# Three moves in the order of VectorE's work: a held bank, a later copy, a longer hand-over

## The chip, the cores and the metric

The kernel runs on one core of a Trainium2 chip. The metric is the time on the device in microseconds (us), the median of several runs. TensorE (PE) multiplies matrices into PSUM banks; VectorE (DVE) and ScalarE (ACT) empty those banks; GpSimd (POOL) works between tiles in SBUF; SyncE (SP) issues the transfers. Each engine works through its own list of instructions in the order in which the program wrote it.

## The reference

Two branches share one input `x` of 2048 rows by 512 columns and are mixed by a gate per row:

```
g = sigmoid((x * gate_w).sum(-1))                     # one number a row
a = attention: 32 heads of width 16, one shared k and v;
    softmax(q k^T / 4) v over all 2048 rows, times wo
b = (silu(x @ w_gate) * (x @ w_up)) @ w_down          # inner width 1792
out = g * a + (1 - g) * b
```

All arrays are 32-bit floats. The 32 heads each need a 2048 x 2048 table of scores and its exponentials; that is the larger part of the work. The feed-forward branch `b` and the queries of the heads are the other part.

## The kernel before, in words

A first stage transposes `x`, splits numbers into a high and a low part (products are made of three terms to keep precision), and makes keys, values and the first queries. A last stage multiplies the attention by `wo`. Between them, from 48.1 to 1289.0 us of the span by its first and last score, lies the attention with the main loop, and the change touches only what is ordered there.

**Blocks.** The main loop first makes 16 short rounds, then one block of another form, and then blocks k = 9 to 127 (line 773). Each unit u is one head and 128 rows of keys. A block makes eight score tiles (two for each of four units, of a later part of the order) and then mixes four units (`mix`, line 665: the exponentials times the values, summed for a head in one bank, `po`). Four blocks make a head, so blocks with k = 0 mod 4 begin one. The order of a block is written out in `STEPS` (line 54): `SSFFFFSFFSFFSFFFSFFFSFFS`. An S makes a score tile, an F feeds one step of other work to TensorE. Steps are counted from 0 here, so the scores 1 to 8 are steps 0, 1, 6, 9, 12, 16, 20, 23, and the sixteen feeds stand between.

**Scores.** A score (line 646) is a pair of matmuls (line 653) on two halves of TensorE's rows into one of two `pss` buffers of two banks each. So a score needs the buffer of the score two before it. `KINDS` (line 55) says how a buffer is emptied: for A, ScalarE takes the exponential of both banks; for H, VectorE copies the second bank out (line 657), ScalarE takes the exponential of the first bank, and later that of the copy. Scores 1, 2, 3, 5 and 6 of a block are H.

**Feeds.** The other work is a list of jobs: query projections, gate and up projections of the feed-forward branch (12 matmuls of 128 rows each), and down projections (15, or 12 in the last group of a chunk). A job fills one of three `pf` banks. `Halves` (line 371) splits each matmul in two of 64 rows, a low and a high half, and runs the low half of one job beside the high half of an earlier one in the same feed (line 175). It keeps a clock: one for each feed, one for each score, 16 for a block's mix. A job's high half may begin `LAG` = 6 clocks after its low half ended; a small VectorE memset of `sign` (line 396) stands between them. When its high half has ended, the bank counts as free `SLACK` = 6 clocks later (line 404), and only then may a new job's low half start on it. No clock of the planner is a time: it only sets the order.

**The end of a job.** With a job's last matmul its `end` is called (line 181), which writes VectorE's operation on the bank: line 260 copies a gate projection out; line 287 multiplies an up projection with the gate's activation (preceded by line 277, if that is not done yet; line 289 where the activation isn't there yet); lines 322 and 324 add a down projection up; lines 208 to 232 are for queries. The functions in `after` then load the next weights. What can wait is put off to the end of the block: the activation on ScalarE (lines 269, 273), and a list `DEFER` of VectorE work with a cost for each (line 277 or 291: 0.7; the cast of the result in two parts, lines 106 and 107: 1.2). A block spends at most `BUDGET` = 3.2 of such cost, and first up to two entries of `LATER`.

**A head's sums.** When a head's last unit is mixed, its bank `po` must be copied out before the next head's first mix, four steps of mixing and eight scores later. That copy (line 690) waits in the list `COPY`, and is written in the next block as soon as two scores are made (line 724), so at step 1, behind score 2. Reciprocals and products (lines 682 to 691) follow through `LATER`.

Of the kernel before, what the change touches and what calls it, by code (L numbers as in the profile page):

```python
# [19 lines left out]
S = 2048  # L20
D = 512
H = 32
# [13 lines left out]
LIMIT = 40.0  # L36
ORDER = (0, 1, 2, 3)
GROUPS = ((0, 1, 2, 3, 4), (5, 6, 7, 8, 9), (10, 11, 12, 13))
SLACK = 6
LAG = 6  # L40
LONG = 8
GAP = 36
# [20 lines left out]
def tile_gated_mix(ctx, tc, x, wq, wk, wv, wo, w_gate, w_up, w_down, gate_w, out):  # L63
# [55 lines left out]
    wg_v = w_gate.rearrange("(k p) f -> p k f", p=P)  # L119
    wu_v = w_up.rearrange("(k p) f -> p k f", p=P)  # L120
    W, HT = {}, {}
    ACTS, DEFER, LOADS = [], [], []

    def run(queue, n):
        for _ in range(min(n, len(queue))):
            queue.pop(0)()
# [30 lines left out]
    def follow(ins, other):  # L157
        tc.add_manual_dep(getattr(ins, "ins", ins), getattr(other, "ins", other).name,
                          mybir.DependencyInfo(mybir.DependencyClass.Sync, mybir.DependencyReason.DATA), reason="rows")

    class Job:
# [4 lines left out]
        def step(self, i, half=None):  # L166
            if i == 0 and not half:
                self.ps = ps_f.tile([P, CH], F32, name="pf")
                self.terms = self.terms()
            a, b = self.terms[i]  # L170
            last = i == self.size - 1
            if half is not None:
                rows = slice(half * RT, (half + 1) * RT)
                a, b = a[rows], b[rows]
            ins = nc.tensor.matmul(self.ps, a, b, start=(i == 0 and not half), stop=(last and half != 0))  # L175
            if half == 0:
                self.lows = ins
            elif half and i == 0:
                follow(ins, self.lows)
            if last and half != 0:  # L180
                self.end(self.ps)
                for f in self.after:
                    f()
                run(LOADS, 2)


    WQ, QS, STORES = {}, {}, []

# [182 lines left out]
    class Halves:  # L371
# [6 lines left out]
        def step(self, more):  # L378
# [20 lines left out]
            if self.high:  # L399
# [3 lines left out]
                if not self.high:  # L403
                    self.free.append(self.clock + SLACK)

# [224 lines left out]
    with tc.tile_pool(name="bpool", bufs=2) as bp:  # L630
# [15 lines left out]
        def score(u, j, half=False):  # L646
            h, kt = divmod(u, NT)
            if j == 0:
                new_pt(u)
            ps = ps_s.tile([P, 2 * CH], F32, name="pss")  # L650
            for b in range(2):
                rows = slice(b * RT, (b + 1) * RT)
                nc.tensor.matmul(ps[:, b * CH:(b + 1) * CH], ks[rows, kt * P:(kt + 1) * P], QS[h][rows, j, :],  # L653
                                 start=True, stop=True)
            halves.clock += 1
            pt = PT[u][:, j * 2 * CH:(j + 1) * 2 * CH]
            other = nc.vector.tensor_copy(pt[:, CH:], ps[:, CH:]) if half else None  # L657
            return pt, ps, other

        def exps(pt, ps, other=None, w=slice(None)):  # L660
            ins = nc.scalar.activation(pt[:, w], ps[:, w], AF.Exp, scale=SCALE)  # L661
            if other is not None:
                tc.declare_no_dep(getattr(ins, "ins", ins), getattr(other, "ins", other), reason="another bank")

        def mix(u):
            h, kt = divmod(u, NT)
            pt = PT.pop(u)
            if kt == 0:
                run(COPY, 1)
                PO[:] = [ps_o.tile([P, CH], F32, name="po")]  # L670
            po = PO[0]
            for c in range(NCH):
                nc.tensor.matmul(po[c * 2 * DH:(c + 1) * 2 * DH, :], vaug[:, kt, :], pt[:, c * CH:(c + 1) * CH],  # L673
                                 start=(kt == 0), stop=(kt == NT - 1))
            if kt == NT - 1:

                osb = hp.tile([P, CH], F32, name="osb")
                rsb = hp.tile([P, CH], F32, name="rsb", bufs=1)

                def invert(i):  # L680
                    w = slice(i * P, (i + 1) * P)
                    nc.vector.reciprocal(rsb[:, w], rsb[:, w])  # L682

                def store():
                    nc.vector.tensor_tensor(osb, osb, rsb, ALU.mult)
                    for c in range(NCH):
                        nc.sync.dma_start(o_d[h * DH:(h + 1) * DH, c * CH:(c + 1) * CH],
                                          osb[c * 2 * DH:c * 2 * DH + DH, :])

                COPY.append(lambda: nc.vector.tensor_copy(osb, po))  # L690
                LATER.extend([(0.8, lambda: nc.vector.stream_shuffle(rsb, osb, [DH] * 2 * DH))] +
                             [(1.0, lambda i=i: invert(i)) for i in range(TC)] + [(0.8, store)])
# [5 lines left out]
        def feed(k, more=True):  # L698
            for _ in range(k):
                if JOBS and more or halves.busy():  # L700
                    halves.step(more)

        def block(k, first, last, steps, kinds, order):
            more = k < NB - STOP
            tiles = [(u, j) for u in range(first, last) for j in range(2)]
            order = list(order)
            made = []

            def emit():
                while order and order[0] != "|" and int(order[0][0]) < len(made):  # L710
                    i, how = int(order[0][0]), order.pop(0)[1]
                    pt, ps, other = made[i]
                    if how == "s":
                        exps(pt, pt, w=slice(CH, None))
                    else:
                        exps(pt, ps, other, slice(0, CH) if kinds[i] == "H" else slice(None))

            for i, what in enumerate(steps):
                if what == "F":
                    feed(1, more)  # L720
                elif len(made) < len(tiles):
                    made.append(score(*tiles[len(made)], kinds[len(made)] == "H"))
                    emit()
                if len(made) > 1:
                    run(COPY, 1)
            if order:
                order.pop(0)
            run(ACTS, len(ACTS))
            emit()
            assert not order and len(made) == len(tiles)  # L730
            left = BUDGET
            for queue, n in ((LATER, 2), (DEFER, len(DEFER))):
                while n and queue and queue[0][0] <= left:
                    cost, f = queue.pop(0)
                    left, n = left - cost, n - 1
                    f()
            for u in range(BLOCK * k, BLOCK * (k + 1)):
                mix(u)
            halves.clock += 2 * LONG
# [7 lines left out]
        with tc.manual_schedule():  # L747
# [25 lines left out]
            for k in range(2 * BEGIN // BLOCK, NB):  # L773
                u = BLOCK * k
                if k == 2 * BEGIN // BLOCK:
                    n = u + 6 - (u + 1)
                    block(k, u + 1, u + 6, TURN, "A" * 2 * n, [f"{i}d" for i in range(2 * n)])
                elif k == NB - 1:
                    block(k, u + 2, u + 4, STEPS, "AAAA", ("0d", "1d", "2d", "3d", "|"))
                else:  # L780
                    block(k, u + 2, u + 6, STEPS, KINDS, EXPS)
                h = u // NT
                if k % (NT // BLOCK) == 0 and 0 < h < H - 1:
                    load_head(h + 1)
                if k == NB - EARLY:
                    load_o(OUTS[0], range(KD - 1))
# [119 lines left out]
```

## Time and profile before

| | us |
|---|---|
| median of three runs | 1374.05 |
| lowest and highest run | 1371.92, 1374.65 |
| the profiled execution | 1375.02 |
| its span, first to last instruction | 1373.3 |
| TensorE busy in the span | 1342.4 (98%) |
| ScalarE busy | 1084.7 (79%) |
| VectorE busy | 867.8 (63%) |
| GpSimd busy | 388.9 (28%) |

The granted clock of TensorE is 0.996 of full speed over the span. Rows of the profile give a line of the kernel, an engine, an operation and its tiles as out<-in. A list in order of time begins each row with start and length in us, counted from the span's start; neighbouring instructions of the same kind are merged into one row with their number behind an x, and in brackets stands the idle time before the row and what ended it. A row of waits reads: who waited <- for whom, us in total, how often, the longest. The table by stretches gives, for each stretch, its length and then the busy time and number of TensorE's matmuls and weight loads. The ends of matmuls are modelled and overlap, so that a busy TensorE may still be waiting.

### The profile page before, as it was taken

Reading aid. Unit: us, or ns where it says so; the run is one execution under the profiler, and the core shown is the slowest. Engines: PE = TensorE matmul, PEld = TensorE weight load, DVE = VectorE, ACT = ScalarE, POOL = GpSimd, SP = SyncE. Lnnn points to the kernel's source line nnn. Section 1 sums busy time; section 2 is a strip of 40 time slices with the busy share of each in tenths; the row PEclk is TensorE's granted clock in tenths of the full one; section 3 lists DMA queues with packets and bytes.
Section 4 is the critical chain, followed back from the end, with each engine's and each line's share of the span. In section 5 each row is a group of like instructions: output and inputs, shape, how many; then the busy total and the mean of one; then the engine's idle time right before and its main releaser. Section 6 shows DMA issues by size and latency. Waiting matters only on the chain. (4 is left out here: it accounts for less than half of the span.)

```text
span 1373.3 us, 27568 instructions
## 1 busy us (share of the span) xinstructions
PE 1342.4 (98%) x10755; PEld 811.2 (59%) x10755; DVE 867.8 (63%) x1458; ACT 1084.7 (79%) x1699; POOL 388.9 (28%) x408
## 2 busy tenths in 40 slices
PE   9999999999999999999999999999999999999998
PEld 7655565565556555656555555655565656565576
DVE  5564677567566667577566676577566666576532
ACT  4578888888888888888888888888888888888500
POOL 6140321142131242142131241241131331332344
PEclk9999999999999999999999999999999999999999
DMA  7456211131141231121141230121221221221154
GB/s 272 144 173 195 79 35 36 41 88 43 51 135 36 66 84 41 47 74 52 51 120 43 71 85 25 58 81 36 59 66 36 81 65 33 74 72 45 44 164 140
DMA packets 101495, 107.84 MB, mean 79 GB/s; under 512 B 9968, under 2 KB 69616, under 8 KB 99696
## 3 DMA queue, kind: packets, MB, share of 16 engines
q1 hardware_dynamic: 99632, 105.81, 26.7%
q8 instruction: 89, 1.46, 0.5%
q10 hardware_dynamic: 1728, 0.20, 0.1%
q14 instruction: 46, 0.38, 0.1%
HBM read 76.09 MB, written 29.36 MB: 77 GB/s over the span
## 5 line engine op out<-in xcount | busy, mean ns | idle before, releaser
L661 ACT ACTIVATE pt<-pss 128x512 f32<-128x512 f32 (+1 forms) x1024 | 757.1, 778 | 183.5 <-PE pss L653 163.9
L657 DVE COPY pt<-pss 128x512 f32<-128x512 f32 x590 | 394.0, 688 | 299.1 <-PE pss L653 293.1
L673 PE MATMUL po<-pt,vaug 128*32 128x512 f32 x4096 | 467.6, 596 | 0.0
L653 PE MATMUL pss<-qs,ks 64*128 64x512 f32 x2048 | 437.6, 421 | 18.1 <-DVE sign L396 5.3
L661 ACT ACTIVATE pt<-pt 128x512 f32<-128x512 f32 x590 | 351.5, 630 | 1.2 <-DVE pt L657 1.2
L653 PEld LDWEIGHTS pss<-qs,ks 64*128 64x128 f32 x2048 | 206.4, 184 | 213.9 <-issue 102.1
L673 PEld LDWEIGHTS po<-pt,vaug 128*32 128x32 f32 x4096 | 119.5, 109 | 272.0 <-issue 271.7
L106 POOL CAST wgh<-wraw 128x512 fp32r<-128x512 f32 x56 | 34.7, 620 | 457.0 <-PE pf L175 368.8
L175 PE MATMUL pf<-xh,wgh 64*128 64x512 f32 (+1 forms) x444 | 164.0, 391 | 0.0
L175 PE MATMUL pf<-xh,wgl 64*128 64x512 f32 (+1 forms) x444 | 162.6, 390 | 0.0
L175 PE MATMUL pf<-xh,wuh 64*128 64x512 f32 (+1 forms) x440 | 162.1, 391 | 0.0
L175 PE MATMUL pf<-xl,wgh 64*128 64x512 f32 (+1 forms) x444 | 161.9, 391 | 0.0
L175 PE MATMUL pf<-xh,wul 64*128 64x512 f32 (+1 forms) x440 | 158.7, 390 | 0.0
L175 PE MATMUL pf<-xl,wuh 64*128 64x512 f32 (+1 forms) x440 | 156.8, 391 | 0.0
L175 PE MATMUL pf<-wdh,hh 64*128 64x512 f32 (+1 forms) x427 | 154.2, 393 | 2.3 <-DVE hh L106 2.0
L175 PE MATMUL pf<-wdl,hh 64*128 64x512 f32 (+1 forms) x427 | 155.2, 393 | 1.0 <-POOL wdl L107 1.0
L175 PE MATMUL pf<-wdh,hl 64*128 64x512 f32 (+1 forms) x427 | 154.0, 392 | 0.0
L682 DVE RECIPROCAL rsb<-rsb 128x128 f32<-128x128 f32 x128 | 116.9, 935 | 3.1 <-issue 0.8
L106 POOL CAST wuh<-wraw 128x512 fp32r<-128x512 f32 x56 | 35.9, 641 | 284.1 <-PE pf L175 248.1
L175 PEld LDWEIGHTS pf<-xh,wgh 64*128 64x128 f32 (+1 forms) x444 | 82.0, 185 | 4.8
L175 PEld LDWEIGHTS pf<-xh,wgl 64*128 64x128 f32 (+1 forms) x444 | 81.6, 185 | 4.3
L175 PEld LDWEIGHTS pf<-xh,wuh 64*128 64x128 f32 (+1 forms) x440 | 81.3, 185 | 4.5
(157 smaller groups left out, 1583.1 us busy)
## 6 DMA issues: line engine op xcount, KB each, us to landing
wraw<-in_B_w_gate_dram SPq DMA_DIRECT2D x56, 256.0 KB
wraw<-in_B_w_up_dram SPq DMA_DIRECT2D x56, 256.0 KB
wraw<-in_B_w_down_dram SPq DMA_DIRECT2D x56, 256.0 KB
qs<-q_d SPq DMA_DIRECT2D x62, 192.0 KB
q_d<-hl SPq DMA_DIRECT2D x18, 256.0 KB
q_d<-hh SPq DMA_DIRECT2D x18, 256.0 KB
o_d<-osb SPq DMA_DIRECT2D x128, 32.0 KB
a_d<-acc SPq DMA_DIRECT2D x4, 1024.0 KB
```

The source lines that it names most:

```text
L106: eng_hi.tensor_copy(hi, src)
L175: ins = nc.tensor.matmul(self.ps, a, b, start=(i == 0 and not half), stop=(last and half != 0))
L653: nc.tensor.matmul(ps[:, b * CH:(b + 1) * CH], ks[rows, kt * P:(kt + 1) * P], QS[h][rows, j, :], start=True, stop=True)
L657: other = nc.vector.tensor_copy(pt[:, CH:], ps[:, CH:]) if half else None
L661: ins = nc.scalar.activation(pt[:, w], ps[:, w], AF.Exp, scale=SCALE)
L673: nc.tensor.matmul(po[c * 2 * DH:(c + 1) * 2 * DH, :], vaug[:, kt, :], pt[:, c * CH:(c + 1) * CH], start=(kt == 0), stop=(kt == NT - 1))
L682: nc.vector.reciprocal(rsb[:, w], rsb[:, w])
```

## The change

`SLACK` goes from 6 to 7. The operation that empties a job's bank, and the functions behind it, move into a new method `leave`, which is put on a list `EVAC`. The list is run at once, except while `HOLD` is set; then it is run behind the next score, its copy included. `HOLD` is set for a feed when one of the next two steps is a score and that score is of kind H. With `STEPS` as it is, these are the feeds at steps 4, 5 (ahead of score 3), 10, 11 (ahead of score 5), 14 and 15 (ahead of score 6). The copy of a head's sums is written when four scores are made, at step 9 in place of step 1.

```diff
-SLACK = 6
+SLACK = 7
...
-    ACTS, DEFER, LOADS = [], [], []
+    ACTS, DEFER, LOADS, HOLD, EVAC = [], [], [], [], []
...
             if last and half != 0:
-                self.end(self.ps)
-                for f in self.after:
-                    f()
+                EVAC.append(self.leave)
+                if not half or not HOLD:
+                    run(EVAC, len(EVAC))
                 run(LOADS, 2)
 
+
+        def leave(self):
+            self.end(self.ps)
+            for f in self.after:
+                f()
...
                 if what == "F":
+                    if "S" in steps[i + 1:i + 3] and kinds[len(made):len(made) + 1] == "H":
+                        HOLD.append(i)
                     feed(1, more)
+                    HOLD.clear()
                 elif len(made) < len(tiles):
                     made.append(score(*tiles[len(made)], kinds[len(made)] == "H"))
                     emit()
-                if len(made) > 1:
+                    run(EVAC, len(EVAC))
+                if len(made) > 3:
                     run(COPY, 1)
```

## The prediction

> **What bounds the kernel now.** I read the page first, then the table of waits, then the engines' lists in order of time for single blocks of the main loop (blocks are numbered by k, lines 773 to 781; score 1 to score 8 are the eight score tiles of a block). Of the page, the span and TensorE's row; of the waits, those of a score's matmul (PE) and of its weight load (PEld):
>
> ```profile
> span 1373.3 us, 27568 instructions
> PE 1342.4 (98%) x10755; PEld 811.2 (59%) x10755; DVE 867.8 (63%) x1458; ACT 1084.7 (79%) x1699; POOL 388.9 (28%) x408
> PEld pss L653 <- issue: 102.1, 125, 0.8
> PEld pss L653 <- ACT pt L661: 88.2, 231, 1.4
> PE pss L653 <- DVE sign L396: 5.3, 10, 0.8
> PE pss L653 <- DVE pt L657: 4.5, 13, 1.0
> ```
>
> TensorE looks full: 1373.3 - 1342.4 = 30.9 us idle. But its queue runs in order, and the score's weight load stands idle 102.1 + 88.2 us, partly while older matmuls still drain. Which wait ends last has to be read in a block. First block 14, VectorE (DVE) and then TensorE, start and length:
>
> ```profile
> 189.96 2.07 DVE L657 COPY pt<-pss 128x512 f32<-128x512 f32 x3 [0.96 <-PE pss L653]
> 192.80 0.69 DVE L657 COPY pt<-pss 128x512 f32<-128x512 f32 x1 [0.27 <-PE pss L653]
> ...
> 189.33 0.73 PE L653 MATMUL pss<-qs,ks 64*128 64x512 f32 x4
> 192.25 0.45 PE L653 MATMUL pss<-qs,ks 64*128 64x512 f32 x2
> ...
> 194.16 0.39 PE L653 MATMUL pss<-qs,ks 64*128 64x512 f32 x2
> ...
> 194.85 0.40 PE L653 MATMUL pss<-qs,ks 64*128 64x512 f32 x2
> 195.18 0.64 PE L673 MATMUL po<-pt,vaug 128*32 128x512 f32 x4
> ```
>
> Scores 1, 2, 3 are copied one behind the other (189.96 to 192.03), score 5 starts at 192.25, score 7 at 194.16, score 8 at 194.85, the mix at 195.18: 2.92 us from score 1 to score 5, 2.93 from there to the mix. Score 5 writes the bank that score 3's copy empties (two pss buffers). Block 12, where a head's sums are copied:
>
> ```profile
> 170.37 1.29 DVE L657 COPY pt<-pss 128x512 f32<-128x512 f32 x2 [2.81 <-PE pss L653]
> 171.57 0.68 DVE L690 COPY osb<-po 128x512 f32<-128x512 f32 x1
> 172.18 0.69 DVE L657 COPY pt<-pss 128x512 f32<-128x512 f32 x1
> ...
> 169.73 0.74 PE L653 MATMUL pss<-qs,ks 64*128 64x512 f32 x4
> 173.01 0.49 PE L653 MATMUL pss<-qs,ks 64*128 64x512 f32 x2 [0.15 <-DVE pt L657]
> 176.00 0.62 PE L673 MATMUL po<-pt,vaug 128*32 128x512 f32 x1
> ```
>
> The L690 copy stands ahead of score 3's copy, which ends at 172.87; score 5 starts 0.14 later: 3.28 + 2.99 us, 0.42 more than block 14. Block 16, where a feed-forward bank's end (L287) stands there too:
>
> ```profile
> 208.78 1.29 DVE L657 COPY pt<-pss 128x512 f32<-128x512 f32 x2 [0.98 <-PE pss L653]
> 209.99 0.68 DVE L690 COPY osb<-po 128x512 f32<-128x512 f32 x1
> 210.58 0.68 DVE L287 TENSOR_TENSOR ht<-ht,pf 128x512 f32<-128x512 f32 x1
> 211.18 0.69 DVE L657 COPY pt<-pss 128x512 f32<-128x512 f32 x1
> ...
> 208.22 0.74 PE L653 MATMUL pss<-qs,ks 64*128 64x512 f32 x4
> 212.01 0.50 PE L653 MATMUL pss<-qs,ks 64*128 64x512 f32 x2 [0.74 <-DVE pt L657]
> 215.00 0.62 PE L673 MATMUL po<-pt,vaug 128*32 128x512 f32 x1
> ```
>
> 3.79 + 2.99 us: 0.93 more than block 14. So each extra operation costs its issue distance of 0.60 (171.57 to 172.18) less a slack of about 0.2 for the first. Sorting blocks 9 to 125 by what stands between the copies of scores 2 and 3 (first 137.5, last 1263.8 us): 58 blocks have nothing there and last 9.44 us on average; 19 the head's copy alone, 9.83 without the odd block 108; 30 a bank's end alone (9.79 with L287, 9.86 with L260, 9.90 with L322 or L324, one of 10.69); 10 both, 9.40 + about 1.0. Over 9.44 this is about 31 us in all: the most that the change can reach.
>
> **The head's copy.** It runs 32 times, and in 29 of the blocks above (12, 16, ... 124):
>
> ```profile
> L690 DVE COPY osb<-po 128x512 f32<-128x512 f32 x32 | 21.8, 682 | 3.3 <-PE po L673 3.3
> L260 DVE COPY hs<-pf 128x512 f32<-128x512 f32 x56 | 38.4, 685 | 20.0 <-PE pf L175 19.8
> L287 DVE TENSOR_TENSOR ht<-ht,pf 128x512 f32<-128x512 f32 x46 | 31.4, 683 | 8.4 <-PE pf L175 7.1
> ```
>
> Now it goes behind score 4, which has no VectorE copy, so between the copies of scores 3 and 5. In block 14 VectorE is free from 192.03 to 192.80: 0.77 us for an issue distance of 0.60, and score 5's copy is not held back. po is wanted again only by the mix, 2.9 us later. Saved: 19 x 0.40 + 10 x 0.57 = 13.3 us. Where a bank's end falls at step 7 or 8 of such a block, two operations stand in the gap: by block 14 score 5's copy would start at 191.95 + 2 x 0.60 = 193.15, end at 193.84, and score 7, which wants that bank, is due at 194.16. Cost taken: nothing, bounds 0 and 29 x 0.4. The page "VectorE: DVE Perf Modes" of the Trainium skill (section on the TRN2 errata) prices a copy out of PSUM at 120 cycles plus one an element, an estimate of 0.66 us for 512; by that price alone 29 copies would give 19 us. The trace has 0.60 between starts, and the first 0.2 of it hidden.
>
> **Holding a bank's end.** It is held only at steps 4, 5 (ahead of score 3), 10, 11 (score 5) and 14, 15 (score 6). The last two cost nothing now: block 46 has L277 and L287 ahead of score 5's copy and lasts 9.54.
>
> ```profile
> 501.88 0.68 DVE L277 SCALAR_TENSOR_TENSOR ht<-ht,hs 128x512 f32<-128x512 f32 x1
> 502.67 0.69 DVE L287 TENSOR_TENSOR ht<-ht,pf 128x512 f32<-128x512 f32 x1
> 503.27 1.28 DVE L657 COPY pt<-pss 128x512 f32<-128x512 f32 x2
> ```
>
> What counts is how many ends fall at steps 4 and 5, and how many at 2 and 3, where nothing is held. In the plan of before 33 of 40 are at 4 and 5 (30 at step 5; counted from the sizes of the jobs and the constants, beside the order of matmuls in the trace), because jobs are 12 feeds long, or 15 four times in a row: ends stay at the last feed of a quarter (steps 5, 11, 17, 22). If that stayed, 33 x 0.35 to 0.46, about 14 us, would go.
>
> **Handing on a bank a step later.** The clock at step s of block k is 40k + s + 10 (24 steps and 16 for the mix). I follow the constants by hand. At step 18 of block 22 a low half starts at clock 908 on a bank free since 902 + 6 = 908; with 7 it starts at step 19. From there all lows are one feed late; the later exact fits (some two dozen in all) are then met. A high half needs the low's end + 6. That has room of one clock at step 19 of block 32: the low ended at step 11, so 1302 + 6 = 1308 against 1309. One feed later it ends at step 13: 1304 + 6 = 1310. The high waits; step 20 is a score; it starts at step 21. So one high half-feed is left empty, and from then on every end comes one feed later: 7, 13, 18 and **step 2 of the next block**. Bank ends shift with it, so lows lose one more feed (block 34), and then the fits hold again. Half-feeds left empty show in the count of L175's matmuls; in four blocks of before from 204.7 us:
>
> ```profile
> 204.70:215.00 10.30, 4.82 (x32) 3.37 (x32) 1.00 0.39 103
> 215.05:224.40 9.35, 4.83 (x29) 3.40 (x29) 1.00 0.01 2
> 224.50:233.75 9.25, 4.79 (x32) 3.31 (x32) 1.00 0.01 2
> 233.85:243.20 9.35, 4.93 (x31) 3.62 (x31) 1.00 0.21 42
> ```
>
> Blocks 17 and 19 leave out three and one, where the constants say so. The missing ones cost no time by themselves (9.35 us). But an end at step 2 is not held, and its operation stands ahead of score 3's copy as it did at step 5. So the hold saves only in blocks 10, 13, 16, 23, 26, 29 (L287, 0.35) and 30 (0.46): 2.6 us. After that 31 such ends (13.8 us) become 27 or so, some eight of them with jobs of 15 or behind block 113: 12.3. Saved there: 1.5.
>
> The shift has a price: L277 is put off to the end of a block, where VectorE's 3.2 us budget takes first the cast of the job before. With ends at 2, 18 and 13, a cast goes in and L277 often doesn't; it is then issued with L287 at step 13, between the copies of scores 5 and 6. Followed by hand this comes 7 times at step 13 (first block 37, last 109) and twice at step 2. Block 59 shows the pair in the worst place, ahead of score 3's copy:
>
> ```profile
> 628.01 0.68 DVE L277 SCALAR_TENSOR_TENSOR ht<-ht,hs 128x512 f32<-128x512 f32 x1
> 628.79 0.69 DVE L287 TENSOR_TENSOR ht<-ht,pf 128x512 f32<-128x512 f32 x1
> 629.40 0.68 DVE L657 COPY pt<-pss 128x512 f32<-128x512 f32 x1
> 194.30 1.68 DVE L277 SCALAR_TENSOR_TENSOR ht<-ht,hs 128x512 f32<-128x512 f32 x1
> ```
>
> 1.39 us for the pair. At step 13, by block 14, score 6's copy would end at 192.80 + 0.60 + 1.39 + 0.69 = 195.48; score 8, due at 194.85, would start 0.77 late with the 0.14 of block 12. Taken: 7 x 0.75 = 5.3 (the two at step 2 are within the 12.3); bounds 0 and 31 (one every three blocks) x 0.75. L277 can also last 1.68 (block 14). The Trainium skill, "SBUF — State Buffer" (Who interferes with whom), says that a VectorE operation with two SBUF inputs and a GpSimd operation lock each other out for a whole instruction; L277 has two, a bank's copy none. POOL is busy 28%, so by that rule 9 pairs would cost some 2 us more. The trace's 1.68 against 0.68 agrees.
>
> A held end also leaves its bank later: in blocks 22 and 25 the next low may wait some 0.3 us each, 0.6 in all.
>
> **Sum.** - 13.3 - 2.6 - 1.5 + 5.3 + 0.6 = - 11.5 us. The profiled execution took 1375.02 (span 1373.3, 1.7 us around it), so 1363.5; the median of the runs, 1374.05, is a microsecond less: **1362**.
>
> **The rivals.** (1) The ends keep to held steps, because the plan slips otherwise than I followed it: then nearly all of the 31 us goes, 1344. For it: the plan fits in two dozen places to the clock, so one slip in a hand count moves the ends. (2) Slower: the L277 and L287 pair. If it comes at step 13 in each of the 31 turns of three blocks, 31 x 0.75 = 23.3 against 16.8 saved by the rest: 1381. It decides from 23 turns on. Against it: blocks with k = 3 mod 4 have the whole budget and clear the queue. (3) The head's copy only moves its wait to scores 7 and 8: 29 x 0.4 = 11.6 comes back, 1374, no change; half of it, 1368. Against it the 0.77 us gap. That ScalarE (79%) comes next is unlikely: blocks without such a wait that follow each other (57 and 58) keep the 9.4 of block 14.
>
> **How the numbers follow.** My sum 0.58, its own range 1355 to 1368; rival 1 0.18; rival 2 0.09; rival 3 whole 0.05, half 0.10. Less than 0.2% (2.7 us) can't be told from no change. Faster is 0.58 + 0.18 + 0.10 = 0.86, same 0.05, slower 0.09. A range of 1345 to 1369 takes in rival 1 and half of rival 3.
>
> **What would show it.** Right: L690 behind the third L657 copy in every fourth block, and those blocks at 9.4 to 9.9; blocks 22, 32 and 34 with 31 matmuls of L175; from block 33 on a bank's end still ahead of score 3's copy in one block of three, now from step 2. Wrong: no empty high half in block 32, ends at step 5 afterwards, or more than some ten L277 and L287 pairs between copies.

## The result, and the profile after

The changed kernel takes 1373.43 us (median of 20 runs, 1369.2 to 1375.95); the kernel before takes 1374.71 in as many (1371.92 to 1376.28). The ratio is 0.9993, with a 95% interval of 0.9986 to 1.0000: no change that can be told. The prediction was 1362, with a range of 1345 to 1369, and 1373.43 lies outside it. Behind the changed lines all line numbers are 5 higher: a score is L658, its copy L662, the exponential L666, the mix L678, the head's copy L695; L265, L282 and L292 are the old L260, L277 and L287; L327 and L329 add up; the mark is L401.

The page of the changed kernel, and from its table of waits those of a score's weight load and of a feed's matmul or weight load (us in total, times, longest):

```profile
span 1373.2 us, 27579 instructions
PE 1344.7 (98%) x10755; PEld 798.9 (58%) x10755; DVE 866.1 (63%) x1458; ACT 1082.0 (79%) x1699; POOL 391.1 (28%) x408
```

```profile
PEld pss L658 <- issue: 106.0, 135, 1.9
PEld pss L658 <- ACT pt L666: 61.2, 216, 2.0
PEld pf L175 <- issue: 14.5, 23, 2.0
PE pf L175 <- DVE ht L292: 6.8, 8, 1.6
PEld pf L175 <- DVE ht L292: 4.5, 6, 1.8
```

The page could be that of the kernel before. The waits couldn't: the score's wait is down from 88.2 to 61.2 us, and feeds, which had next to none, now wait for VectorE and for the queue behind such a wait. A saving and a loss of the same size stand against each other. The saving is in block 12, VectorE and then TensorE:

```profile
171.35 1.29 DVE L662 COPY pt<-pss 128x512 f32<-128x512 f32 x2 [2.94 <-PE pss L658]
172.73 0.69 DVE L662 COPY pt<-pss 128x512 f32<-128x512 f32 x1
173.34 0.68 DVE L695 COPY osb<-po 128x512 f32<-128x512 f32 x1
174.19 0.69 DVE L662 COPY pt<-pss 128x512 f32<-128x512 f32 x1 [0.17 <-PE pss L658]
...
170.71 0.74 PE L658 MATMUL pss<-qs,ks 64*128 64x512 f32 x4
173.64 0.44 PE L658 MATMUL pss<-qs,ks 64*128 64x512 f32 x2
...
176.64 0.64 PE L678 MATMUL po<-pt,vaug 128*32 128x512 f32 x4
```

L695 stands behind the third copy, score 5's copy still waits for its score (0.17), and from score 1 to score 5 it is 2.93 us in place of 3.28; from there to the mix 3.00.

**Where the time went.** To see the rest I took blocks 9 to 125 of each trace and measured the distance between the starts of neighbouring scores. Less the shortest usual distance of each stretch (from score 4 to 5 it is 0.69, from 5 to 6 0.92, from 6 to 7 0.93, from 7 to 8 0.69, from the mix to score 1 3.57) and summed over the blocks, in us:

| kernel | blocks 9 to 125 | score 4 to 5 | 5 to 6 | 6 to 7 | 7 to 8 | mix to score 1 |
|---|---|---|---|---|---|---|
| before | 1135.7 | 27.1 | 5.6 | 0.7 | 1.6 | 0.0 |
| after | 1134.7 | 7.0 | 6.0 | 8.0 | 10.7 | 1.7 |

The stretch in front of score 5 gave 20.1 us. Of this 7.3 came back ahead of score 7, 9.1 ahead of score 8, 1.7 at the start of block 120 and 0.4 ahead of score 6. Both losses can be read in one block each.

**A held bank is late.** Block 68, where L265 empties a bank whose job ended at step 10; it is held until score 5 and its copy are written. VectorE, then TensorE:

```profile
715.32 0.69 DVE L662 COPY pt<-pss 128x512 f32<-128x512 f32 x1 [0.16 <-PE pss L658]
715.93 0.68 DVE L265 COPY hs<-pf 128x512 f32<-128x512 f32 x1
716.53 0.68 DVE L662 COPY pt<-pss 128x512 f32<-128x512 f32 x1
...
715.71 0.42 PE L658 MATMUL pss<-qs,ks 64*128 64x512 f32 x2
...
716.66 0.49 PE L175 MATMUL pf<-wdh,hh 64*128 64x512 f32 x1 [0.30 <-DVE hs L265]
...
717.23 0.40 PE L658 MATMUL pss<-qs,ks 64*128 64x512 f32 x2
```

The next job's low half (`wdh`, 716.66) takes that bank two steps behind score 6. It starts 0.05 behind the end of L265 (716.61), TensorE's queue stops with it, and from score 6 (715.71) to score 7 (717.23) it is 1.52 us in place of 0.93. Fourteen blocks lose 0.37 to 0.74 in this stretch: 22, 25, 65, 68, 71, 74, 77, 86, 89, 98, 101, 104, 107 and 110. Blocks 55 and 58 lose 0.6 one stretch later.

**A pair is dear.** Block 46: VectorE, GpSimd and TensorE.

```profile
500.27 0.69 DVE L662 COPY pt<-pss 128x512 f32<-128x512 f32 x1 [0.77 <-PE pss L658]
500.88 1.66 DVE L282 SCALAR_TENSOR_TENSOR ht<-ht,hs 128x512 f32<-128x512 f32 x1
502.65 0.69 DVE L292 TENSOR_TENSOR ht<-ht,pf 128x512 f32<-128x512 f32 x1
503.25 0.68 DVE L662 COPY pt<-pss 128x512 f32<-128x512 f32 x1
...
500.00 0.62 POOL L106 CAST wuh<-wraw 128x512 fp32r<-128x512 f32 x1 [6.05 <-PE pf L175]
500.70 1.30 POOL L107 TENSOR_TENSOR wul<-wraw,wuh 128x512 fp32r<-128x512 f32 x1
...
501.62 0.40 PE L658 MATMUL pss<-qs,ks 64*128 64x512 f32 x2
503.48 0.47 PE L175 MATMUL pf<-xh,wgh 64*128 64x512 f32 x1 [1.47 <-DVE ht L292]
504.08 0.49 PE L658 MATMUL pss<-qs,ks 64*128 64x512 f32 x2
```

L282 takes 1.66 us beside GpSimd's subtraction L107, so L292 ends at 503.34. The low half of the next job waits 1.47 us for that bank, and from score 7 (501.62) to score 8 (504.08) it is 2.46 us in place of 0.69. Blocks 46, 49, 119 and 122 lose 1.76 to 1.97 us ahead of score 8, block 37 0.79. Elsewhere a pair costs some 0.74 (block 39, ahead of score 5: 1.07 against 0.33 with the end alone), 0.87 (111) and 0.28 (59), and block 120, behind the pair of block 119, starts 1.67 late: eight pairs, 11.6 us in all, by blocks. Six more pairs (14, 17, 27, 67, 79 and 109) stand behind the last copy of their block and cost next to nothing.

The count of feeds shows how the plan went. L175's matmuls in blocks 22, 32, 34 and 50:

```profile
261.60:271.20 9.60, 4.99 (x31) 3.16 (x31) 1.00 0.00 0
357.60:367.20 9.60, 4.82 (x31) 3.49 (x31) 1.00 0.19 41
376.80:386.10 9.30, 4.92 (x31) 3.37 (x31) 1.00 0.12 30
535.10:544.30 9.20, 4.76 (x31) 3.23 (x31) 1.00 0.00 0
```

The first three were followed by hand and are there. The fourth was not: it moves the ends on, from steps 2, 7, 13, 18 to 3, 8, 14, 19, and further empty halves in 54, 61, 65, 94, 98, 116 and 117 move them on again. From block 61 to 93 they fall at 4, 10, 15 and 21, of which 4, 10 and 15 are held.

### The profile page after: what moved, and what is told of

The parts are those of the page before. It is cut to its first block, busy times and chain, and to the rows that moved or that the text cites. A ratio compares the mean times of both kernels' runs of the same rounds, so it can differ in the third digit from the quotient of the medians.

```text
span 1373.2 us, 27579 instructions
## 1 busy us (share of the span) xinstructions
PE 1344.7 (98%) x10755; PEld 798.9 (58%) x10755; DVE 866.1 (63%) x1458; ACT 1082.0 (79%) x1699; POOL 391.1 (28%) x408
## 5 line engine op out<-in xcount | busy, mean ns | idle before, releaser
L666 ACT ACTIVATE pt<-pss 128x512 f32<-128x512 f32 (+1 forms) x1024 | 753.9, 778 | 185.2 <-PE pss L658 166.5
L662 DVE COPY pt<-pss 128x512 f32<-128x512 f32 x590 | 395.4, 688 | 312.2 <-PE pss L658 295.9
L678 PE MATMUL po<-pt,vaug 128*32 128x512 f32 x4096 | 469.3, 597 | 0.0
L658 PE MATMUL pss<-qs,ks 64*128 64x512 f32 x2048 | 432.7, 418 | 5.9 <-DVE pt L662 4.0
L666 ACT ACTIVATE pt<-pt 128x512 f32<-128x512 f32 x590 | 351.8, 630 | 1.4 <-DVE pt L662 1.3
L658 PEld LDWEIGHTS pss<-qs,ks 64*128 64x128 f32 x2048 | 202.6, 184 | 197.4 <-issue 106.0
L678 PEld LDWEIGHTS po<-pt,vaug 128*32 128x32 f32 x4096 | 119.5, 110 | 272.1 <-issue 272.1
L175 PE MATMUL pf<-xh,wgh 64*128 64x512 f32 (+1 forms) x444 | 167.5, 394 | 5.0 <-DVE ht L292 4.4
L175 PE MATMUL pf<-xh,wuh 64*128 64x512 f32 (+1 forms) x440 | 167.2, 393 | 2.9 <-DVE sign L401 0.7
L175 PE MATMUL pf<-xl,wgh 64*128 64x512 f32 (+1 forms) x444 | 169.7, 390 | 0.0
L175 PE MATMUL pf<-xh,wgl 64*128 64x512 f32 (+1 forms) x444 | 169.3, 395 | 0.0
L175 PE MATMUL pf<-xh,wul 64*128 64x512 f32 (+1 forms) x440 | 167.2, 394 | 0.0
L175 PE MATMUL pf<-xl,wuh 64*128 64x512 f32 (+1 forms) x440 | 163.0, 390 | 0.0
L175 PE MATMUL pf<-wdl,hh 64*128 64x512 f32 (+1 forms) x427 | 158.2, 392 | 2.4 <-POOL wdl L107 2.4
L175 PE MATMUL pf<-wdh,hh 64*128 64x512 f32 (+1 forms) x427 | 157.5, 394 | 2.9 <-DVE ht L292 2.4
L175 PE MATMUL pf<-wdh,hl 64*128 64x512 f32 (+1 forms) x427 | 156.9, 392 | 0.0
L175 PEld LDWEIGHTS pf<-xh,wgh 64*128 64x128 f32 (+1 forms) x444 | 81.2, 185 | 16.4 <-issue 6.4
L175 PEld LDWEIGHTS pf<-xh,wuh 64*128 64x128 f32 (+1 forms) x440 | 80.9, 184 | 12.8 <-issue 7.2
L175 PEld LDWEIGHTS pf<-wdh,hh 64*128 64x128 f32 (+1 forms) x427 | 79.0, 186 | 12.7 <-DVE ht L292 4.5
```

## The experiments

Each is an edit of the kernel before or of the changed one. Ratios are to the kernel before on the same chip, with a 95% interval; "the table" is the one by stretches above, continued here for the runs:

| run | blocks 9 to 125 | score 4 to 5 | 5 to 6 | 6 to 7 | 7 to 8 |
|---|---|---|---|---|---|
| copy_alone | 1121.3 | 14.6 | 4.3 | 1.2 | 1.5 |
| slack_alone | 1146.1 | 27.5 | 5.6 | 0.0 | 12.2 |
| hold_alone_6 | 1150.2 | 13.5 | 13.3 | 19.9 | 2.5 |
| copy_and_hold_6 | 1136.7 | 3.0 | 10.5 | 19.8 | 1.7 |
| copy_and_slack_7 | 1131.5 | 15.2 | 4.2 | 0.1 | 12.0 |
| hold_first_6 | 1116.1 | 3.2 | 11.3 | 1.1 | 1.5 |
| hold_first_7 | 1123.6 | 7.1 | 6.1 | 0.1 | 11.1 |
| pairs_split | 1120.8 | 8.3 | 4.0 | 3.0 | 4.6 |
| slack_pairs_split | 1134.0 | 24.9 | 5.2 | -0.2 | 1.8 |
| pairs_beside_casts | 1128.4 | 7.1 | 6.2 | 8.2 | 7.4 |
| hold_quarter_6 | 1111.5 | 1.0 | 10.3 | 1.3 | 1.4 |
| hold_quarter_7 | 1124.3 | 19.2 | 2.2 | 0.2 | 1.8 |

### The parts, each alone

The later copy alone, in the kernel before:

```diff
-                if len(made) > 1:
+                if len(made) > 3:
                     run(COPY, 1)
```

> Only the head's copy is moved (four scores in place of two); SLACK stays 6 and nothing is held. Theory A (the terms of the change are separate, and the head's copy is worth its stall of 0.40 to 0.57 us in 29 blocks): 13 us less than before, about 1361. Rival B (the copy takes its wait along to scores 7 and 8): 1374, with those scores 0.3 to 0.4 us late in every fourth block.

1360.31 us, ratio 0.9898 (0.9881 to 0.9914): 14.0 us saved (0.0102 x 1374). The stretch from score 4 to 5 falls from 27.1 to 14.6, and nothing comes back behind it. In its waits a score's weight load stands 77.2 us where it stood 88.2, and the feeds wait no more than before:

```profile
PEld pss L653 <- ACT pt L661: 77.2, 242, 1.4
PEld pf L175 <- issue: 0.8, 1, 0.8
```

The longer hand-over alone, in the kernel before:

```diff
-SLACK = 6
+SLACK = 7
```

> Only SLACK 7: nothing held, the head's copy where it was. Theory A (the shifted order brings pairs of L277 and L287 ahead of score 6's copy, which in the changed kernel cost 0.8 to 2 us in blocks 37, 46, 49, 119 and 122): about 8 us more than before, 1382, and half-feeds empty in blocks 22, 32, 34, 50, 54, 61, 65, 94, 98, 116, 117. Rival B (the order is as good as that of before, the loss in the changed kernel is all from held banks): 1374.

1385.32 us, ratio 1.0076 (1.0060 to 1.0093): 10.4 us lost, all of it ahead of score 8 (1.6 to 12.2). Seven blocks make up 10.1 us of this (37, 46, 49, 67, 79, 119 and 122), and each has a pair between the copies of scores 5 and 6. Block 46 of this run has the same pair as the changed kernel:

```profile
505.43 1.67 DVE L277 SCALAR_TENSOR_TENSOR ht<-ht,hs 128x512 f32<-128x512 f32 x1
507.20 0.69 DVE L287 TENSOR_TENSOR ht<-ht,pf 128x512 f32<-128x512 f32 x1
```

So the place of the pairs comes from the constant and not from the hold: in the kernel before, the pair of block 46 stands ahead of score 5's copy and costs nothing. The hold alone, the changed kernel with the old hand-over and the old place of the copy:

```diff
-SLACK = 7
+SLACK = 6
...
-                if len(made) > 3:
+                if len(made) > 1:
                     run(COPY, 1)
```

> Only the hold, with SLACK 6 and the head's copy where it was. The ends stay at steps 5, 11, 17, 22, so 33 stalls of score 5 go (14 us). Theory A (a held bank is late for the next low half): in 23 turns a bank that ended at step 11 is wanted at step 18 and comes 0.6 us late (13.8), in 22 turns one that ended at step 5 is wanted at step 13 and comes 0.3 late (7.5): 7 us more than before, about 1381. Rival B (the hold costs nothing, what ate the gain is the planner's new order): 1360.

1386.95 us, ratio 1.0089 (1.0073 to 1.0106): the hold by itself costs 12 us, more than either theory had. It does what it was followed to do ahead of score 5 (27.1 to 13.5), and gives 19.2 us back ahead of score 7 and 7.7 ahead of score 6. The old hand-over with the other two parts:

```diff
-SLACK = 7
+SLACK = 6
```

> The whole change with SLACK 6 in place of 7. Theory A (held banks are waited for; the order of before kept): - 13 - 14 + 21 = 6 us less than before, about 1368. Rival B (only the order that SLACK 7 makes ate the gain): 13 + 14 = 27 us less, about 1347.

1376.83 us, ratio 1.0019 (1.0008 to 1.0029), above both figures. Its waits show what I had missed of size: the feeds' waits for L292 and for the queue behind it.

```profile
PEld pf L175 <- issue: 18.8, 31, 2.3
PE pf L175 <- DVE ht L292: 8.4, 13, 1.8
PEld pf L175 <- DVE ht L292: 6.3, 5, 2.2
```

A bank held from step 11 to behind score 5 is wanted by the low half at step 18, some 0.65 us too early (blocks 22, 25, 34 and others); one held from step 5 to behind score 3 is wanted at step 13, 0.36 too early. Where a pair is held at step 11 (blocks 46, 70 and 79), it costs 2.0 to 2.1. So two of the three parts lose by themselves, and more than the first saves: 12.2 + 10.4 - 14.0 would be 8.6 us more than before, where the changed kernel takes 1 us less. The parts don't add up. With the copy moved, the hold costs 16.6 us at a hand-over of 6 (0.9898 to 1.0019) and, as the run without it will show, 1.8 at 7: with 6 there are 23 blocks that lose ahead of score 7 behind a held bank, with 7 fourteen.

### The hold ahead of score 3 only

If the loss ahead of score 7 is due to the banks held behind score 5, it must go when only those behind score 3 are held. With both hand-overs (the run with 6 sets `SLACK` back as well):

```diff
-                    if "S" in steps[i + 1:i + 3] and kinds[len(made):len(made) + 1] == "H":
+                    if "S" in steps[i + 1:i + 3] and len(made) == 2 and kinds[2] == "H":
                         HOLD.append(i)
```

> The head's copy moved, SLACK 6, and a bank's end held only ahead of score 3 (steps 4 and 5), no longer ahead of scores 5 and 6. Theory A (a hold gains at score 3 and costs where the bank is wanted next; measured in the run with the whole hold and SLACK 6: score 5 loses 11.6 us of waiting against the copy alone, the banks held at step 5 cost 6.2 between scores 5 and 6, those held at 10 and 11 cost 18.6 between scores 6 and 7): 1360.3 - 11.6 + 6.2 = 1355. Rival B (the wait for the bank is set by VectorE's load and not by the hold, so it stays): 1373 to 1377.

> The changed kernel (SLACK 7, copy moved) with the hold only ahead of score 3. Theory A: the waits between scores 6 and 7 and 7 and 8 behind banks held at steps 10, 11, 14 and 15 (17 blocks, 0.37 to 0.74 each, 9 us) go: 1364. Rival B (they are the order's own): 1373.

1354.24 us with 6, ratio 0.9855 (0.9839 to 0.9872), and 1364.08 with 7, ratio 0.9917 (0.9901 to 0.9934). The stretch from score 6 to 7 falls from 19.8 to 1.1 and from 8.0 to 0.1, while that from score 4 to 5 stays (3.0 to 3.2, 7.0 to 7.1). The banks held behind scores 5 and 6 are the cause of the loss ahead of score 7; by the rows it is those behind score 5. With 7, blocks 55 and 58 lose nothing either, and the sum ahead of score 8 stays (10.7 to 11.1) because the pairs of blocks 67 and 79, which the hold had put behind the last copy, cost 1.1 each here. The third run leaves the hold out: it is the kernel before with the longer hand-over and the later copy, without `EVAC` and `HOLD`.

```diff
-SLACK = 6
+SLACK = 7
...
-                if len(made) > 1:
+                if len(made) > 3:
                     run(COPY, 1)
```

> The changed kernel without any hold: copy moved, SLACK 7. Theory A (terms add): 1385.3 - 14.7 = 1370.6, so the hold in the changed kernel costs 3 us net. Rival B (the hold is a gain, and copy and SLACK hinder each other): above 1375.

1371.47 us, ratio 0.9980 (0.9970 to 0.9989): some 2 us less than with the hold, though the two intervals still overlap a little. In the changed kernel the hold gains 8.2 ahead of score 5 (15.2 to 7.0) and loses 7.9 ahead of score 7 (0.1 to 8.0), with a little more elsewhere.

### The pairs

L282 joins the end of its own job, two operations together, because it was put off and found no room in the block's budget. With a cost of nothing it always goes at the end of a block:

```diff
-                    DEFER.append((0.7, silu))
+                    DEFER.append((0.0, silu))
```

> The changed kernel, with cost 0 in place of 0.7 for L277 in the list of put-off work, so that it is done at the end of its block and does not come with L287 inside the next. Theory A (the pairs in blocks 37, 39, 46, 49, 59, 111, 119, 122 cost 11.6 us with block 120's late start): 1373.4 - 11.6 = 1362, S7 to S8 back from 10.7 to under 3 us in all. Rival B (the work only moves to the end of the block and holds up the next block's first copies): 1373, with scores 2 and 3 later.

> SLACK 7 alone, as in the run above that took 1385.3, and cost 0 for L277 in the put-off work. Theory A (all that SLACK 7 costs by itself are the pairs of L277 and L287 at step 13; between scores 7 and 8 it has 12.2 us of waiting, before has 1.6): 1375. Rival B (it costs by the order in general): 1382 or more.

In the changed kernel (pairs_split) 1361.94 us, ratio 0.9902 (0.9885 to 0.9918); in the kernel before with `SLACK` = 7 (slack_pairs_split) 1374.69, ratio 1.0002 (0.9992 to 1.0011). No pair is left in either run. In the second, all that the longer hand-over lost is regained (12.2 to 1.8 ahead of score 8). The first regains 12.5 us. Neither run tests the pairs alone, since the edit also moves the plan: behind block 34, L175's matmuls show the next empty half-feed in block 92 and no longer in block 50. So the ends stay at step 2 longer. In the second run this changes the stretch ahead of score 5 little (27.5 to 24.9); in the first, the late banks of blocks 65 to 89 go with it (8.0 to 3.0 ahead of score 7), so part of the 12.5 is theirs.

Why a pair costs twice what I took: in the changed kernel `load_split` casts `w_up` on GpSimd and then subtracts for the low part. Here the low part of `w_up` is made by a second cast, of one input, in place of the subtraction of two. So the kernel leaves out the remainder of `w_up` and has the rounded `w_up` a second time in its place.

```diff
-    def load_split(view, name, bufs, pool=wp):
+    def load_split(view, name, bufs, pool=wp, copy=False):
...
+        if copy:
+            nc.gpsimd.tensor_copy(hi, raw)
+            nc.gpsimd.tensor_copy(lo, raw)
+            return hi, lo
...
-                W[nm, n] = load_split({"g": wg_v, "u": wu_v}[nm][:, :, fs], "w" + nm, 2)
+                W[nm, n] = load_split({"g": wg_v, "u": wu_v}[nm][:, :, fs], "w" + nm, 2, copy=nm == "u")
```

> The changed kernel, with the low part of w_up replaced by a second cast on GpSimd (one input, 0.62 us, in place of the subtraction with two inputs, 1.30 us), so the products leave out the correction for w_up. Theory A (L277 waits on GpSimd's subtraction, which the same last matmul sets free): L277 inside blocks 46, 49, 119 and 122 takes under 1.0 us in place of 1.65 to 1.82, and the run some 4 us less, 1369. Rival B (it waits for something else): as long as before, 1373.

1368.96 us, ratio 0.9968 (0.9954 to 0.9982). Block 46 again, VectorE and GpSimd (lines 4 higher than in the changed kernel), and under them the L282 of the changed kernel as a group (shortest, median and longest in ns):

```profile
499.67 0.83 DVE L286 SCALAR_TENSOR_TENSOR ht<-ht,hs 128x512 f32<-128x512 f32 x1
500.60 0.69 DVE L296 TENSOR_TENSOR ht<-ht,pf 128x512 f32<-128x512 f32 x1
...
498.79 0.61 POOL L140 CAST wuh<-wraw 128x512 fp32r<-128x512 f32 x1 [6.04 <-PE pf L179]
499.34 0.62 POOL L141 CAST wul<-wraw 128x512 fp32r<-128x512 f32 x1
```

```profile
L282 DVE SCALAR_TENSOR_TENSOR ht<-ht,hs x52: 679/692/1822, 129.9 to 1305.9; 128x512 f32<-128x512 f32 x52
```

The pair is still there, and the operation takes 0.83 in place of 1.66 (0.81 to 0.88 in blocks 46, 49, 119 and 122). Ahead of score 8 it is 7.4 in place of 10.7. So the price of a pair has two parts: its place between the copies, and the GpSimd instruction beside it, which is shorter here.

### A version that beats both

What the runs point to: the old hand-over, the later copy, no pairs, and only the ends ahead of score 3 held, but those of all four feeds there (steps 2 to 5). Against the changed kernel:

```diff
-SLACK = 7
+SLACK = 6
...
-                    DEFER.append((0.7, silu))
+                    DEFER.append((0.0, silu))
...
-                    if "S" in steps[i + 1:i + 3] and kinds[len(made):len(made) + 1] == "H":
+                    if len(made) == 2 and kinds[2] == "H":
```

> SLACK 6, the head's copy moved, every bank's end at steps 2 to 5 held behind score 3 and none elsewhere, and cost 0 for L277 in the put-off work. Theory A: against the run that holds only at steps 4 and 5 (1354.2), seven blocks with ends at steps 2 and 3 lose 0.45 each and block 59 its late bank of 2.1 us: 1349. Rival B (an end held for so long makes its bank late, or L277 at a block's end holds up the next one): 1354 or more.

1350.43 us, ratio 0.9827 (0.9810 to 0.9843): 24 us less than the kernel before and 23 less than the changed one. From score 4 to 5 only 1.0 us is left, and a score's weight load waits 50.9 us for the exponential, 88.2 before; what is left of note is 10.3 ahead of score 6. Most of what the hold at steps 2 and 3 gains ahead of score 5 comes back there: blocks 31, 32, 53, 94, 95 and 116, which lost 0.34 to 0.40 ahead of score 5 in hold_first_6, lose 0.14 to 0.43 ahead of score 6. Block 59's 2.1 us are gone.

```profile
span 1348.2 us, 27575 instructions
PE 1331.5 (99%) x10755; PEld 801.0 (59%) x10755; DVE 859.6 (64%) x1458; ACT 1078.2 (80%) x1699; POOL 387.9 (29%) x408
PEld pss L658 <- ACT pt L666: 50.9, 186, 1.4
```

The same with the longer hand-over:

```diff
-                    DEFER.append((0.7, silu))
+                    DEFER.append((0.0, silu))
...
-                    if "S" in steps[i + 1:i + 3] and kinds[len(made):len(made) + 1] == "H":
+                    if len(made) == 2 and kinds[2] == "H":
```

> The run before (ends at steps 2 to 5 held behind score 3, cost 0 for L277, copy moved) with SLACK 7 in place of 6. Theory A (without pairs and without banks held in the rest of a block SLACK itself is worth nothing, apart from later lows meeting their banks): from the run with the hold at steps 4 and 5 and SLACK 7 (1364.1), 9.6 less for the pairs between scores 7 and 8 and some 4 less between scores 4 and 5: 1350, within 3 us of the same with SLACK 6. Rival B (SLACK 7 costs in another way too): 1357 or more.

1362.46 us, ratio 0.9911 (0.9894 to 0.9927): 12 us more than without the longer hand-over, so the theory that had 1350 falls. Block 36 shows where, VectorE and TensorE:

```profile
395.91 2.07 DVE L662 COPY pt<-pss 128x512 f32<-128x512 f32 x3 [0.98 <-PE pss L658]
397.90 0.68 DVE L292 TENSOR_TENSOR ht<-ht,pf 128x512 f32<-128x512 f32 x1
398.50 0.69 DVE L695 COPY osb<-po 128x512 f32<-128x512 f32 x1
398.52 0.06 DVE L401 MEMSET sign<- 1x1 f32 x1
...
397.52 0.43 PE L658 MATMUL pss<-qs,ks 64*128 64x512 f32 x2
398.73 0.47 PE L175 MATMUL pf<-xh,wgh 64*128 64x512 f32 x1 [0.78 <-DVE sign L401]
...
399.26 0.43 PE L658 MATMUL pss<-qs,ks 64*128 64x512 f32 x2
```

With 7, the ends lie mostly at step 2 from block 33 to 91. The end of step 2, L292, is now held behind three copies and ends at 398.58. Its bank is free in the plan at step 10, right behind score 4 (397.52), and the low half that takes it starts at 398.73. The profile names the mark L401, which ends in the same 398.58; the bank is what a low half needs, by the code. In all 18 such waits the operation that empties a bank ends in the same hundredth as the mark. Score 5 comes 1.74 us behind score 4 in place of 0.69. The waits sum it up: 18 times, 12.9 us.

```profile
PE pf L175 <- DVE sign L401: 12.9, 18, 0.9
```

The run pairs_split settles the reading: it has the same plan, and differs only in which ends are held. Steps 2 and 3 are not among them, so in block 36 L292 stands ahead of score 3's copy:

```profile
399.95 0.68 DVE L292 TENSOR_TENSOR ht<-ht,pf 128x512 f32<-128x512 f32 x1
400.54 0.69 DVE L662 COPY pt<-pss 128x512 f32<-128x512 f32 x1
401.17 0.06 DVE L401 MEMSET sign<- 1x1 f32 x1
...
400.77 0.46 PE L175 MATMUL pf<-xh,wgh 64*128 64x512 f32 x1
```

The low half starts without a wait, 0.40 before the mark, so it doesn't need the mark. Score 5 comes 1.02 us behind score 4, and the stretch is 8.3 us in all where it is 19.2 with the hold at steps 2 and 3.

With 6, the ends are at step 5 mostly and their bank is wanted at step 13: there the hold costs 6.0 us ahead of score 6 (4.3 in copy_alone to 10.3) and gains 13.6 ahead of score 5.

## Why the prediction was wrong

**The head's copy: right.** 13.3 us was the sum, 14.0 the measurement. It cost nothing elsewhere: rival 3, by which its wait only moves, had 11.6 us coming back ahead of scores 7 and 8, where copy_alone has 1.2 and 1.5.

**The plan: right up to block 50, then wrong.** The empty halves in blocks 22, 32 and 34 and the ends at steps 2, 7, 13 and 18 are as followed. (By the code the clock is 40k + s + 12, two more than taken, which changes no comparison of two clocks.) The step that failed is "and then the fits hold again". They don't: the first job of 15 feeds behind that point starts in block 49, its high half comes due one clock too late in block 50, and seven more empty halves follow. The ends pass through all places in turn. That is why the hold gained 8.2 us ahead of score 5 and not 4.1 (2.6 + 1.5): from block 61 to 93 the ends were at step 4, and five behind block 94 at step 5, and were held again. It is also why rival 1, ends that keep to held steps, wasn't the case either. That this saving came out larger than the sum had it is luck.

**The held banks: mis-sized, 0.6 taken, 7.9 measured.** That "in blocks 22 and 25 the next low may wait some 0.3 us each" names the right mechanism; those two lost 0.41 and 0.44. But I only followed it where the ends of the old plan were, at step 11, and asked only what stands between the copies. A hold behind score 5 gives the bank to the low half of steps 18 or 19, whose matmuls TensorE reaches before VectorE is through with two copies and the held operation. With the ends at steps 10 and 11, that is in 14 blocks, and 12 of them (65 to 110) lie behind block 50, where the plan had gone another way: the failed step of the plan is what made this term so large. Another 1.8 ahead of score 6 and 1.2 in blocks 55 and 58 are late banks too. The runs with 6 show the whole size: 19.2 us.

**The pairs: the count about right, the price not.** I took 7 at step 13 with 0.75 each, 5.3 us. There are five that cost ahead of score 8 (37, 46, 49, 119, 122) and three in other places (39, 59, 111). That the count came near is partly luck, since 119 and 122 belong to the part of the plan that was not followed rightly. Block 37 lost 0.79, as priced; the other four lost 1.76 to 1.97, and all eight together, with the late start of block 120, 11.6. The sentence on the "1.68 (block 14)" had the cause in hand and gave it "some 2 us more" from GpSimd's 28%. An average was the wrong measure: the last matmul of an up projection ends the job, and so calls L282 and L292, and in the same moment frees the `wu` buffer for which GpSimd's cast and subtraction wait (`[6.05 <-PE pf L175]` in block 46). So the two meet far more often than by chance: ten of the 14 pairs have an L282 of over a microsecond, and two of the 38 that are no part of a pair. Rival 2 had this as the way to a slower kernel, with 31 pairs at 0.75: the mechanism is there, with fewer pairs at more than twice the price where GpSimd is beside them.

**The sum.** Taken in this order, as measured: - 14.0 for the copy, + 10.4 for the longer hand-over with its pairs, + 1.8 for the hold on top of both (ratio 0.9980 without it, 0.9993 with it), so - 1.8 against - 1.0 by the ratio. The rest is within the intervals. In another order the terms differ, as the runs with 6 show. The expected gain was there, and two mechanisms that the prediction names gave it back because both were sized too small.

## What to carry to other kernels

When an operation that empties a buffer is put off on an engine that works in order, price it by who takes the buffer next and when, not only by what it stood in front of; the two runs that held only ahead of score 3 differ from those that held everywhere by this alone. A constant with a margin of one in a plan moves everything behind the first misfit, so follow such a plan to its end or don't forecast from it. And price an operation in the company it will have: where one event releases work on two engines, they meet far more often than their average use says.

## What the runs showed of the hardware

VectorE's operation with two SBUF inputs waits for the end of a whole GpSimd instruction that started before it. In the changed kernel 12 of 52 L282 take over a microsecond, 1.32 to 1.82, against 0.69 for most. Each of the 12 starts 0.02 to 0.52 us behind the start of an L107, which takes 1.3, and each ends 0.55 behind its end. Block 46 shows it: L107 ends at 502.00, L282 at 502.54. The kernel before has 8 of 46, 1.2 to 1.72, each again 0.55 behind the end of an L107. GpSimd's cast, with one input, does the same and is only shorter: in block 46 of the run with two casts the cast ends at 499.96 and the operation at 500.50, and no wait for a cast makes it longer than 0.91 in that run. The other way round GpSimd waits: where L282 starts first (430.56 in the changed kernel) it takes 0.68, and the cast that starts 0.17 behind it takes 0.98 in place of 0.61. The Trainium skill, "SBUF — State Buffer" (Who interferes with whom), says that a VectorE instruction with two SBUF inputs contends with a GpSimd instruction that reads SBUF, and that the ports that the two share are an exclusive lock. The trace agrees, and adds that the price is the rest of GpSimd's instruction, up to 1.1 us here.

TensorE's busy share told nothing of what could be won: it is 98% in both kernels, and 99% in the version that takes 24 us less than the kernel before. What showed the gain was the distance between scores, stretch by stretch.
